# Attention, then a feed-forward network with Strassen-Winograd products: preparing the last part earlier, and a piece of a plain block kept to cover it

## The chip, the cores and the metric

The kernel runs on one core of a Trainium2 chip. The core has a matrix engine (TensorE, PE in the profile; its weight loads are PEld), a vector engine (VectorE, DVE), a scalar engine (ScalarE, ACT), a general engine (GpSimd, POOL) and an engine that only issues transfers (SyncE, SP). Each takes its instructions in its own order, and engines wait for each other by semaphores. Matrix products go into PSUM, which here has two large banks ("sc") and four small ones ("mm") in turn; everything else is kept in SBUF. The metric is the time of one execution in microseconds of device time, the median of three runs.

## The reference

64 attention heads (batch 8 x 8 heads) of 576 rows and 64 columns, in which only scores within tau of a row's largest take part, and then a feed-forward network on all 4608 rows:

```python
scores = scale * np.matmul(q, k.transpose(0, 1, 3, 2))
thresh = np.max(scores, axis=-1, keepdims=True) - tau
scores = np.where(scores >= thresh, scores, -1000000000.0)
scores = scores - np.max(scores, axis=-1, keepdims=True)
attn = np.exp(scores)
attn = attn / (np.sum(attn, axis=-1, keepdims=True) + 1e-09)
attn_out = np.matmul(attn, v)
# (B,H,S,D) -> (B*S, H*D)
x = attn_out.transpose(0, 2, 1, 3).reshape(4608, 512)
h = x @ w_in                       # 512 x 2048
g = 0.5 * h * (1.0 + erf(h / np.sqrt(2)))
out = g @ w_out                    # 2048 x 512
```

All in float32.

## The kernel before

The 4608 rows of x are 18 blocks of 256. Blocks 0 to 7 go through the network in the plain way (`block_steps`: products hT, gelu, products o_ps); their products fill PE between the scores of attention, since attention keeps DVE busy. Blocks 8 to 17 come after attention, as two groups of five blocks, in the last part: there both layers are done by the Strassen-Winograd scheme, with 7 products of quarters instead of 8, in two levels for the first layer. That needs sums of quarters of x, of the weights and of g, made by DVE and GpSimd.

Attention goes by pairs of heads (32 of them) and by 5 chunks of rows for each. A chunk's scores go into the "sc" banks (one for each head), DVE takes their maxima, ScalarE the exponentials, and DVE's last pass sets what lies under the threshold to zero and sums the rows. Only then can the next chunk's scores go in. How much of a plain block is put between is set by a table of goals, in blocks (a block is some 54.6 us of PE):

```python
GOAL = [(-1, 0.0), (START - 1, 0.0), (BATCH - 1, 0.42)]
GOAL += [(BATCH * (m + 2) + DIVIDE, x) for m, x in enumerate([1.96, 2.97, 3.98, 4.98, 5.99, 6.99])]
GOAL += [(BATCH * B + WEIGH, PLAIN)]
...
fill(1e12, B * S)          # what is left of the plain blocks, after attention
late_end.close()
last_blocks()
```

At the end of each pair the row sums are turned, inverted and spread over the partitions by way of DRAM (`divisors`), the weighted sum of v goes to x (`weigh_v`, products xT, copied by ScalarE), and GpSimd multiplies it by the inverses (`divide`):

```python
def divisors(p):
    ...
    nc.vector.transpose(turned, den)
    rows = dram.tile([4, Q, Q], FP32, tag="turned", name="turned", bufs=4)
    nc.sync.dma_start(rows.rearrange("a k i -> (a k) i"), turned)
    t = st[p]["inv"] = dg.tile([P, S], FP32, tag="inv", name="inv")
    ...                                    # four more, rows -> t, on nc.sync
```

The last part begins with the sums of x (t_x, x and, in place, xall) and of w_out (t_out); the sums of w_in (s_in, s_out, s_plain) have been issued after the last scores. What stands in `beside` is issued piece by piece, one piece after each product (`step`):

```python
x_tiles()
beside.extend(x_sums())
for _ in range(9):
    beside.pop(0)[1]()
w_out_sums(vec, 0)
```

A step (group n, quarter j of the hidden columns; 8 steps in all) does a first layer and a second. A chain of seven products adds up in its banks: m1 is evicted, m6 is added on top and evicted again, then m5, then m3, each into another quarter of the result; m7 and m4 do the same in a second bank. m5 and m3 of a chain are issued among the products of the next one (`before`).

```python
def chain(n, m, takes, done=None, runs=1):
    x, y = bank("sc", n), bank("mm", n)
    ...
    step(one_of("m1", x, True))
    step(before[0])                        # m5 of the chain before
    step(one_of("m7", y, True))
    if v is not None:
        step(one_of("m2", v, True))
    step(before[1])                        # m3 of the chain before
    step(one_of("m6", x, False))
    step(one_of("m4", y, False))
    waiting.append((one_of("m5", x, False), one_of("m3", x, False)))
```

The first layer is seven such chains of 49 products; the last two make V = c[:, 2] (g12) and U = c[:, 1] (g21), and R and W are g11 and g22:

```python
outer("a12", "b21", R, R, when(m3=lambda: (gelu_on(flat(W)), gelu_on(flat(R)))))
outer("a22", "t4", V, V, when(m3=lambda: gelu_on(flat(V))))

last = {"m2": lambda: gelu_on(U[:, 0, 0, :]), "m4": lambda: gelu_on(U[:, 1, 0, :]),
        "m5": lambda: gelu_on(U[:, 1, 1, :]), "m3": lambda: gelu_on(U[:, 0, 1, :])}
outer("s4", "b22", U, U, when(**last))
```

The second layer begins with five products of g12, among them m5 and m3 of the last chain, then come five chains of six. DVE adds each product to the output o (`taken`; in the first step of a group ScalarE copies it instead, where there is nothing yet to add to). The sums of g (8 of them, 128 x 640; the first is g21 + g22 of the first half) are issued beside:

```python
for m in range(MT):
    v = bank("mm", HD)

    def run(m=m, v=v):
        product(v, rows(g12, m, w(1, 0)), True)
        taken(lo[m][:, 0:HD], v, None if first else lo[m][:, 0:HD])

    step(run)
    if m < 2:
        step(before[m])                    # m5, then m3 of the last chain
    if m == 1:
        sums = list(g_sums())
        beside.extend(sums[:3])
        beside.extend(spread(sums[3:]))    # spread: every second step
between(-1)
for m in range(MT):
    ...
    chain(HD, ms, takes, done)
    between(m)
```

Of the kernel before, what the change touches and what calls it, by code (L numbers as in the profile page):

```python
# [18 lines left out]
def kernel(  # L19
# [28 lines left out]
    nc = tc.nc  # L48
    ctx.enter_context(tc.manual_schedule())

    B, H, S, D = q.shape
    d_model, d_ff = moe_w_in.shape
    P = 128
    Q = 32
    HP = H // 2
    NP = B * HP
    EARLY = HP
    NC = S // P
    MAIN = NC * P
# [390 lines left out]
    def divisors(p):  # L450

        den = sums[p % 2]
        n = 2 * NC + 1
        nc.vector.tensor_scalar(den[:, 0:n], den[:, 0:n], 1e-9, None, op0=ALU.add)
        nc.vector.reciprocal(den[:, 0:n], den[:, 0:n])
        turned = small.tile([P, Q], FP32, tag="turned", name="turned", bufs=2)
        nc.vector.transpose(turned, den)
        rows = dram.tile([4, Q, Q], FP32, tag="turned", name="turned", bufs=4)  # L460
        nc.sync.dma_start(rows.rearrange("a k i -> (a k) i"), turned)
        t = st[p]["inv"] = dg.tile([P, S], FP32, tag="inv", name="inv")
        flat = rows.rearrange("a k i -> a (k i)")
        for e in range(2):
            to = t[e * D:(e + 1) * D]
            src = flat[:, e * P:(e + 1) * P].unsqueeze(0).to_broadcast([D, 4, P])
            nc.sync.dma_start(to[:, 0:MAIN].rearrange("p (a x) -> p a x", x=P), src)
            src = rows[2 * e:2 * e + 2, 2 * NC, :].unsqueeze(0).to_broadcast([D, 2, Q])
            nc.sync.dma_start(to[:, MAIN:S].rearrange("p (a x) -> p a x", x=Q), src)

    def turn_p(p, i):

# [189 lines left out]
    def sub(eng, out, a, b):  # L662
        eng.tensor_tensor(out, a, b, op=ALU.subtract)  # L663
# [83 lines left out]
    def x_sums():  # L747

        room = list(tail["x_room"])
        x = xall[:, 0:len(AWAY), :, :].rearrange("p b (k h) (o t) -> p b k h o t", k=2, o=2)  # L750
        part = {f"b{k + 1}{o + 1}": x[:, :, k, :, o, :] for k in range(2) for o in range(2)}
        right = tail["right"] = {}

        def inner(eng, name, v, keep=False):
            b = {(h, i): v[:, :, h, i * RUN:(i + 1) * RUN] for h in range(2) for i in range(2)}
            t1, t2, t4 = (room.pop(0) for _ in range(3))
            t3 = room.pop(0) if keep else b[0, 1]
            right[name] = {"b11": b[0, 0], "b21": b[1, 0], "b22": b[1, 1], "t1": t1, "t2": t2, "t3": t3, "t4": t4}
            yield eng, lambda: sub(eng, t1, b[0, 1], b[0, 0])
            yield eng, lambda: sub(eng, t3, b[1, 1], b[0, 1])  # L760
            yield eng, lambda: sub(eng, t2, b[1, 1], t1)
            yield eng, lambda: sub(eng, t4, b[1, 0], t2)

        def outer(eng, out, a, b):
            yield eng, lambda: sub(eng, out, a, b)

        t1, t2, t4 = tail["t_x"]
        yield from outer(vec, t1, part["b12"], part["b11"])
        yield from inner(vec, "b11", part["b11"])
        yield from inner(vec, "t1", t1, True)  # L770
        yield from outer(vec, t2, part["b22"], t1)
        yield from inner(vec, "t2", t2, True)
        yield from outer(vec, part["b12"], part["b22"], part["b12"])
        yield from inner(vec, "t3", part["b12"])
        yield from inner(vec, "b22", part["b22"])
        yield from outer(vec, t4, part["b21"], t2)
        yield from inner(pool, "b21", part["b21"])
        yield from inner(pool, "t4", t4)
# [21 lines left out]
    def step(which):  # L800

        if which is not None:
            which()
        if beside:
            beside.pop(0)[1]()
        while beside and beside[0][0] is pool:
            beside.pop(0)[1]()
# [26 lines left out]
    def gelu_on(t):  # L834
        nc.scalar.activation(t, t, AF.Gelu)  # L835

    def layer_in(j, between):

        c, g = tail["c"], tail["g"]
        R, U, V, W, T = c[:, 0], c[:, 1], c[:, 2], c[:, 3], g[:, 0]  # L840

        def flat(t):
            return t.rearrange("p a b c -> p (a b c)")

        def outer(a, b, to, first, done=None):
            l, r = left(a, j), tail["right"][b]
            m = {"m1": ("a11", "b11"), "m2": ("a12", "b21"), "m3": ("s4", "b22"), "m4": ("a22", "t4"),
                 "m5": ("s1", "t1"), "m6": ("s2", "t2"), "m7": ("s3", "t3")}
            m = {k: [(l[p], r[q])] for k, (p, q) in m.items()}

            def at(f, t, again=False):
                d = to[:, f, t, :]
                return d, (d if again else None if first is None else first[:, f, t, :])

            takes = {"m1": [at(0, 0)], "m7": [at(1, 1)], "m6": [at(1, 0)], "m4": [at(1, 0, True)],
                     "m2": [at(0, 0, True)], "m5": [at(1, 1, True)], "m3": [at(0, 1)]}
            chain(QT, m, takes, done, len(AWAY))

        def when(**what):
            return lambda name: what[name]() if name in what else None  # L860

        def m5_out(f, t):
            return lambda: add(pool, W[:, f, t, :], V[:, f, t, :], T[:, f, t, :])

        def m5_all():
            m5_out(0, 1)()
            add(pool, flat(U), flat(U), flat(T))

        outer("a11", "b11", R, None)
        outer("s1", "t1", T, None)  # L870
        between()
        outer("s2", "t2", U, R)
        outer("s3", "t3", V, U, when(m2=m5_out(0, 0), m4=m5_out(1, 0), m5=m5_out(1, 1), m3=m5_all))
        outer("a12", "b21", R, R, when(m3=lambda: (gelu_on(flat(W)), gelu_on(flat(R)))))
        outer("a22", "t4", V, V, when(m3=lambda: gelu_on(flat(V))))

        last = {"m2": lambda: gelu_on(U[:, 0, 0, :]), "m4": lambda: gelu_on(U[:, 1, 0, :]),
                "m5": lambda: gelu_on(U[:, 1, 1, :]), "m3": lambda: gelu_on(U[:, 0, 1, :])}
        outer("s4", "b22", U, U, when(**last))

    def g_sums():

# [16 lines left out]
    def layer_out(blocks, j, between, first, final):  # L899
# [19 lines left out]
# [4 lines that stand above are left out]
                product(v, rows(g12, m, w(1, 0)), True)  # L923
                taken(lo[m][:, 0:HD], v, None if first else lo[m][:, 0:HD])

            step(run)
            if m < 2:
                step(before[m])
            if m == 1:
                sums = list(g_sums())  # L930
                beside.extend(sums[:3])
                beside.extend(spread(sums[3:]))
        between(-1)
        for m in range(MT):
            l0, l1, h0, h1 = lo[m][:, 0:HD], lo[m][:, HD:2 * HD], hi[m][:, 0:HD], hi[m][:, HD:2 * HD]
# [14 lines left out]
    def last_blocks():  # L950

        assert set(x_free) == {XSLOTS - 2, XSLOTS - 1}
        GROUPS[0].sort(key=x_at.get)
        x_tiles()
        beside.extend(x_sums())
        for _ in range(9):
            beside.pop(0)[1]()
        w_out_sums(vec, 0)
        steps = [(n, j if n % 2 == 0 else NJ - 1 - j) for n in range(len(GROUPS)) for j in range(NJ)]
        for at, (n, j) in enumerate(steps):  # L960
            before = steps[at - 1] if at else None
            after = steps[at + 1] if at + 1 < len(steps) else None

            def in_layer_in():
                if before and before[1] != j:
                    w_out_sums(pool, j)

            def in_layer_out(m):
                if after is None:
                    return  # L970
                if m == -1 and after[0] != n:
                    for k in range(2):
                        for b, x in enumerate(GROUPS[after[0]]):
                            nc.sync.dma_start(xall[:, b, 2 * k:2 * k + 2, :], away[x][:, 2 * k:2 * k + 2, :])
                if m == 0 and after[1] != j:
                    beside.append((pool, lambda j=after[1]: w_in_sums(pool, j)))
                if m == 2 and after[0] != n:
                    beside.extend(x_sums())

            layer_in(j, in_layer_in)  # L980
            layer_out(GROUPS[n], j, in_layer_out, at % NJ == 0, at % NJ == NJ - 1)
        while waiting:
            for f in waiting.pop(0):
                f()
        assert not beside
# [29 lines left out]
    START = 2 * HP + 2  # L1015

    GOAL = [(-1, 0.0), (START - 1, 0.0), (BATCH - 1, 0.42)]
    GOAL += [(BATCH * (m + 2) + DIVIDE, x) for m, x in enumerate([1.96, 2.97, 3.98, 4.98, 5.99, 6.99])]
    GOAL += [(BATCH * B + WEIGH, PLAIN)]

    def goal(n):
        for (lo, x), (hi, y) in zip(GOAL, GOAL[1:]):
# [134 lines left out]
```

## Time and profile before

| what | value |
|---|---|
| time, median of 3 | 1376.94 us (1376.78 to 1378.49) |
| span of the profiled run | 1375.6 us |
| granted clock of PE, mean | 0.992 |
| last scores of attention begin | 872.65 us |
| first product of the last part begins | 891.38 us |
| second group's first product begins | 1132.97 us |
| PE busy from 240 to 840 us | 598.85 of 600 us |
| DVE busy from 240 to 840 us | 506.57 of 600 us |

The timeline gives for each run of instructions its start and duration in us, its engine and line, what it writes and reads with the shapes, how many there are, and in square brackets how long the engine had been idle before it and on whose instruction that ended. A float32 product of the program appears as two PE records. PE's ends are modelled and reach over into the next product, so what a product costs is read from start to start. The waits give for pairs of instructions the total in us, the number of times and the longest.

### The profile page before, as it was taken

The numbers are of one execution on the slowest core, as the hardware profiler recorded it, in microseconds if no ns is written. First come the engines' busy times: TensorE is split into PE (matmuls) and PEld (weight loads), VectorE is DVE, ScalarE is ACT, GpSimd is POOL, SyncE is SP. The second block draws the span as 40 slices with busy tenths as digits, with TensorE's granted clock in tenths as the row PEclk, the third lists the DMA queues.
The fourth block names the chain that finished last, engine by engine and source line by source line (L and its number), as shares of the span: only waits on it lengthen the run. The fifth ranks groups of instructions, "written<-read, shape, count | busy, mean of one in ns | idle before, by whom it ended". The sixth has DMA issues, their size and how long they took to land.

```text
span 1375.6 us, 20037 instructions
## 1 busy us (share of the span) xinstructions
PE 1341.1 (97%) x6398; PEld 903.3 (66%) x6398; DVE 1064.8 (77%) x2054; ACT 599.6 (44%) x1000; POOL 629.3 (46%) x1080
## 2 busy tenths in 40 slices
PE   9899999999999999999999999989999999999998
PEld 6677557466466466466466476458787776877776
DVE  7998777788888888888888888883857678375665
ACT  7766537448348358358367357222201102211120
POOL 5553344455554554554554551136264403635430
PEclk9999999999999999999999999999999999999999
DMA  9987366577677687787787776500000140000003
GB/s 294 318 305 218 79 160 142 140 165 177 158 171 177 156 194 171 156 211 166 160 202 168 160 178 135 120 1 1 0 1 0 39 100 16 1 1 0 1 0 77
DMA packets 213255, 169.18 MB, mean 123 GB/s; under 512 B 114256, under 2 KB 194448, under 8 KB 213152
## 3 DMA queue, kind: packets, MB, share of 16 engines
q1 hardware_dynamic: 189200, 112.84, 37.5%
q0 software_dynamic: 23520, 54.77, 12.9%
q8 instruction: 52, 0.85, 0.3%
q14 instruction: 51, 0.42, 0.1%
q10 hardware_dynamic: 432, 0.30, 0.1%
HBM read 72.73 MB, written 12.52 MB: 62 GB/s over the span
## 4 chain that ended last, share of the span: by engine, by line
PE 87%; DVE 6%; ACT 3%; DMA 2%; issue 1%; SPq 0%; POOL 0%; ACTq 0%; DVEq 0%; POOLq 0%
PE bank L782 30%; PE hT L596 16%; PE o_ps L611 16%; PE sc L403 13%; PE xT L520 10%; PE tr L345 2%; ACT c L835 1%; DVE o L666 1%; ACT p L418 1%; DVE nmx L415 1%; DVE p L434 1%; DVE c L666 1%; DMA turned_p<-in_moe_w_in_dram 1%; DVE t_x L663 0%; DVE g L666 0%
## 5 line engine op out<-in xcount | busy, mean ns | idle before, releaser
L418 ACT ACTIVATE p<-sc,nmx 128x576 f32<-128x576 f32 x288 | 201.7, 737 | 266.9 <-DVE nmx L415 266.7
L434 DVE SCALAR_TENSOR_TENSOR p<-sc,thr,p 128x576 f32<-128x576 f32 x288 | 225.2, 815 | 62.5 <-ACT p L418 59.0
L416 POOL TENSOR_SCALAR thr<-nmx,tau_eff 128x1 f32<-128x1 f32 x288 | 89.0, 309 | 387.2 <-DVE nmx L415 386.6
L415 DVE TENSOR_REDUCE nmx<-sc 128x1 f32<-128x576 f32 x288 | 205.5, 750 | 65.5 <-PE sc L403 64.7
L596 PE MATMUL hT<-xall,w_in 128*128 128x256 f32 x1024 | 241.1, 385 | 0.0
L611 PE MATMUL o_ps<-w_out,g 128*128 128x512 f32 x512 | 237.6, 604 | 0.0
L596 PEld LDWEIGHTS hT<-xall,w_in 128*128 128x128 f32 x1024 | 189.5, 190 | 49.2 <-issue 23.8
L666 DVE TENSOR_TENSOR o<-o,bank 128x256 f32<-128x256 f32 x240 | 100.3, 419 | 106.8 <-PE bank L782 102.9
L666 DVE TENSOR_TENSOR c<-c,bank 128x320 f32<-128x320 f32 x304 | 147.2, 487 | 38.9 <-PE bank L782 23.8
L611 PEld LDWEIGHTS o_ps<-w_out,g 128*128 128x128 f32 x512 | 93.3, 190 | 111.1 <-issue 109.5
L520 PE MATMUL xT<-pT,v 128*64 128x256 f32 (+1 forms) x1280 | 163.9, 409 | 0.6 <-issue 0.6
L403 PE MATMUL sc<-kT,qT 64*128 64x288 f32 x960 | 157.5, 431 | 2.6 <-DVE p L434 2.1
L481 DVE STREAM_TRANSPOSE turned_p<-p 128x1152 f32<-128x1152 f32 x112 | 154.4, 1378 | 3.9
L403 PEld LDWEIGHTS sc<-kT,qT 64*128 64x128 f32 x960 | 89.4, 187 | 76.4 <-issue 64.8
L520 PEld LDWEIGHTS xT<-pT,v 128*64 128x64 f32 x1280 | 89.0, 137 | 73.0 <-issue 12.8
L782 PE MATMUL bank<-w_out,c 128*128 128x256 f32 x480 | 121.1, 383 | 8.0 <-ACT c L835 6.9
L265 POOL DMA_DIRECT2D v<-in_v_dram x208 | 110.8, 536 | 4.5 <-issue 2.7
L782 PEld LDWEIGHTS bank<-w_out,c 128*128 128x128 f32 x480 | 89.2, 190 | 29.3 <-ACT c L835 10.9
L835 ACT ACTIVATE c<-c 128x320 f32<-128x320 f32 (+1 forms) x56 | 44.6, 810 | 116.2 <-POOL c L666 67.8
L793 ACT COPY c<-bank 128x320 f32<-128x320 f32 x32 | 13.6, 425 | 166.3 <-PE bank L782 166.1
L782 PE MATMUL bank<-t_out,g 128*128 128x256 f32 x320 | 82.8, 381 | 1.2 <-DVE o L666 1.2
L782 PE MATMUL bank<-t_out,c 128*128 128x256 f32 x320 | 83.1, 382 | 0.0
(178 smaller groups left out, 1825.0 us busy)
## 6 DMA issues: line engine op xcount, KB each, us to landing
pT<-turned_p SPq DMA_DIRECT2D x448, 160.0 KB, 3.7
pT<-pd_tail SPq DMA_DIRECT2D x112, 80.0 KB, 3.0
q<-in_q_dram POOLq DMA_DIRECT2D x104, 72.0 KB, 3.3
k<-in_k_dram POOLq DMA_DIRECT2D x104, 72.0 KB, 3.2
inv<-turned SPq DMA_DIRECT2D x56, 128.0 KB, 3.9
v<-in_v_dram POOLq DMA_DIRECT2D x156, 40.0 KB, 3.3
out_dram<-o SPq DMA_DIRECT2D x40, 128.0 KB, 2.4
xall<-in_moe_w_out_dram POOLq DMA_DIRECT2D x9, 512.0 KB, 4.0
```

The lines of the kernel that those rows point to most:

```text
L265: eng.dma_start(t[r:P:4, e, 0:n, :], rows[:, r * KR:r * KR + n, :])
L403: nc.tensor.matmul(sc[e][:, h, 0:HALF], lhsT=lhsT, rhs=s["kT"][rows, at:at + HALF], start=True, stop=True)
L415: nc.vector.tensor_reduce(nmx[:, e:e + 1], sc, axis=AXIS.XY, op=ALU.max, negate=True)
L416: nc.gpsimd.tensor_scalar(thr[:, e:e + 1], nmx[:, e:e + 1], -1.0, tau_eff, op0=ALU.mult, op1=ALU.subtract)
L418: nc.scalar.activation(w[:, e * S:(e + 1) * S].rearrange("p (h s) -> p h s", h=2), sc, AF.Exp, bias=nmx[:, e:e + 1], scale=1.0)
L434: nc.vector.scalar_tensor_tensor(row, sc[e][:, :, 0:HALF], thr[:, e:e + 1], row, op0=ALU.is_ge, op1=ALU.mult, accum_out=den[e])
L481: nc.vector.transpose(turned_p[:, :, i // 2, 0:NB, i % 2 * Q:(i % 2 + 1) * Q], w.rearrange("p (e b i) -> p e b i", e=2, i=Q))
L520: nc.tensor.matmul(to, lhsT=s["v"][:, e, c, :], rhs=rhs, start=(c == 0), stop=(c == KR - 1))
L596: nc.tensor.matmul(hT[:, j % 2, :], lhsT=w_in_sb[c][:, j * P:(j + 1) * P], rhs=x_blk[n][:, c, :], start=(c == 0), stop=(c == N_DM - 1))
L611: nc.tensor.matmul(o[:, 0:d_model], lhsT=g[j][:, m * P:(m + 1) * P], rhs=w_out_sb[j], start=(j == 0), stop=(j == N_DF - 1))
L666: eng.tensor_tensor(out, a, b, op=ALU.add)
L782: nc.tensor.matmul(to, lhsT=l, rhs=r, start=start and k == 0, stop=k == len(pairs) - 1, skip_group_check=not start)
```

## The change

It has five pieces. The last pair's divisors are issued by GpSimd's queue, as SyncE's is full of transfers there. The goals of the plain blocks are lower, so that 0.28 of the last plain block is left for after attention, where its products can run while the sums for the last part are made; these are all issued ahead of the last part, not piece by piece between its products. The gelu of g12 is done in four quarters, each as soon as it is complete. The first sum of g is issued before the first product of the second layer. And the second group's x sums are issued from the second row of products on, not from the fourth, with each large one (`outer`) in two halves.

```diff
+        eng = nc.gpsimd if p == NP - 1 else nc.sync
         rows = dram.tile([4, Q, Q], FP32, tag="turned", name="turned", bufs=4)
-        nc.sync.dma_start(rows.rearrange("a k i -> (a k) i"), turned)
+        eng.dma_start(rows.rearrange("a k i -> (a k) i"), turned)
 ...                                       (the four others likewise)
         def outer(eng, out, a, b):
-            yield eng, lambda: sub(eng, out, a, b)
+            for h in range(2):
+                yield eng, lambda h=h: sub(eng, out[:, :, h, :], a[:, :, h, :], b[:, :, h, :])
 ...
-        outer("a22", "t4", V, V, when(m3=lambda: gelu_on(flat(V))))
-
-        last = {"m2": lambda: gelu_on(U[:, 0, 0, :]), "m4": lambda: gelu_on(U[:, 1, 0, :]),
-                "m5": lambda: gelu_on(U[:, 1, 1, :]), "m3": lambda: gelu_on(U[:, 0, 1, :])}
-        outer("s4", "b22", U, U, when(**last))
+
+        def gelus_of(to):
+            return when(**{m: lambda f=f, t=t: gelu_on(to[:, f, t, :])
+                           for m, f, t in (("m2", 0, 0), ("m4", 1, 0), ("m5", 1, 1), ("m3", 0, 1))})
+
+        outer("a22", "t4", V, V, gelus_of(V))
+        outer("s4", "b22", U, U, gelus_of(U))
 ...
+            if m == 0:
+                sums = list(g_sums())
+                sums.pop(0)[1]()
             step(run)
             if m < 2:
                 step(before[m])
             if m == 1:
-                sums = list(g_sums())
-                beside.extend(sums[:3])
-                beside.extend(spread(sums[3:]))
+                beside.extend(sums[:2])
+                beside.extend(spread(sums[2:]))
 ...
-        beside.extend(x_sums())
-        for _ in range(9):
-            beside.pop(0)[1]()
+        sums = list(x_sums())
+        for _, run in sums[:10]:
+            run()
         w_out_sums(vec, 0)
+        for _, run in sums[10:]:
+            run()
 ...
-                if m == 2 and after[0] != n:
+                if m == 0 and after[0] != n:
                     beside.extend(x_sums())
 ...
-    GOAL += [(BATCH * (m + 2) + DIVIDE, x) for m, x in enumerate([1.96, 2.97, 3.98, 4.98, 5.99, 6.99])]
-    GOAL += [(BATCH * B + WEIGH, PLAIN)]
+    GOAL += [(BATCH * (m + 2) + DIVIDE, x) for m, x in enumerate([1.92, 2.89, 3.86, 4.82, 5.79, 6.75])]
+    GOAL += [(BATCH * B + WEIGH, PLAIN - 0.28)]
```

More of the change, by code (lines that the diff above doesn't have):

```diff
@@ L466, in divisors @@
             src = flat[:, e * P:(e + 1) * P].unsqueeze(0).to_broadcast([D, 4, P])
-            nc.sync.dma_start(to[:, 0:MAIN].rearrange("p (a x) -> p a x", x=P), src)
+            eng.dma_start(to[:, 0:MAIN].rearrange("p (a x) -> p a x", x=P), src)
             src = rows[2 * e:2 * e + 2, 2 * NC, :].unsqueeze(0).to_broadcast([D, 2, Q])
-            nc.sync.dma_start(to[:, MAIN:S].rearrange("p (a x) -> p a x", x=Q), src)
+            eng.dma_start(to[:, MAIN:S].rearrange("p (a x) -> p a x", x=Q), src)
     def turn_p(p, i):
```

## The prediction

> **What bounds the kernel now.** I read the page first, then the waits of the matrix engine (PE) alone, then its timeline wherever those waits fall. The page gives PE 97% busy:
>
> ```profile
> PE 1341.1 (97%) x6398; PEld 903.3 (66%) x6398; DVE 1064.8 (77%) x2054; ACT 599.6 (44%) x1000; POOL 629.3 (46%) x1080
> ```
>
> No matmul is removed by this change, so all it can win is time in which PE stands still or runs at a lower clock: 1375.6 - 1341.1 = 34.5 us of idle, and some of that is the start. The waits of PE, each with its total, its count and its longest:
>
> ```profile
> PE bank L782 <- ACT c L835: 6.9, 8, 0.9
> PE tr L345 <- ACT diag L448: 5.7, 2, 3.6
> PE bank L782 <- DVE c L666: 5.4, 1, 5.4
> PE sc L403 <- DVE p L434: 3.0, 4, 1.6
> PE bank L782 <- DVE o L666: 3.0, 9, 0.7
> ```
>
> Rows 1, 3 and 5 lie in the last part (line 782), and the change aims at them. Row 2 is the start and stays. Row 4 is attention. The timeline of PE at the hand-over from attention to the last part:
>
> ```profile
> 895.15 0.70 PE L782 MATMUL bank<-x,s_out 128*128 128x320 f32 x2
> 895.69 0.70 PE L782 MATMUL bank<-t_x,s_out 128*128 128x320 f32 x2
> 901.83 1.43 PE L782 MATMUL bank<-xall,s_plain 128*128 128x320 f32 x2 [5.44 <-DVE c L666]
> 903.06 1.27 PE L782 MATMUL bank<-x,s_in 128*128 128x320 f32 x2
> 904.12 1.27 PE L782 MATMUL bank<-x,s_out 128*128 128x320 f32 x2
> ```
>
> A product normally starts 0.54 us after the one before it. Here one starts 6.14 us after (5.6 lost), and the next ones step by 1.07 until 907.3: 901.83 to 907.92 is 6.09 us for six steps that cost 3.24 (2.85 lost). One more gap at 908.85 loses 0.39. Sum 8.8 us. The timeline where a first layer of the last part goes over into its second:
>
> ```profile
> 1100.04 0.70 PE L782 MATMUL bank<-x,s_out 128*128 128x320 f32 x2
> 1101.61 1.13 PE L782 MATMUL bank<-w_out,c 128*128 128x256 f32 x4 [0.87 <-ACT c L835]
> 1102.57 0.70 PE L782 MATMUL bank<-x,s_in 128*128 128x320 f32 x2
> 1103.11 1.03 PE L782 MATMUL bank<-w_out,c 128*128 128x256 f32 x4
> 1103.97 0.70 PE L782 MATMUL bank<-xall,s_in 128*128 128x320 f32 x2
> ...
> 1099.74 2.17 ACT L835 ACTIVATE c<-c 128x320 f32<-128x320 f32 x3 [2.02 <-DVE c L666]
> ...
> 1102.77 0.42 DVE L666 TENSOR_TENSOR o<-o,bank 128x256 f32<-128x256 f32 x1 [1.46 <-PE bank L782]
> 1103.31 0.49 DVE L666 TENSOR_TENSOR c<-c,bank 128x320 f32<-128x320 f32 x1
> ```
>
> PE could start at 1100.04 + 0.54 = 1100.58 and starts at 1101.61: 1.03 lost, plus 0.1 for a slower first product. ScalarE is then in the 1.27 us gelu of g12, which it began after a small one. DVE stands idle 1.46 us before 1102.77. This occurs in each of the 8 steps.
>
> [...] 1.07 us for each product after the 5.44 us wait, 0.54 otherwise; the waits of 0.9 us show no such thing. [...] a gelu of 128x320 takes 0.47 us and one of 128x1280 takes 1.27, so four take 1.88. [...] SyncE issues 16 + 1 + 4 transfers from 867.0 to 884.3 while the divisors have been ready since 877.6.
>
> **The change part by part.**
>
> *Part of a block behind attention.* I counted in the order of instructions what fills PE between one chunk's scores and the next, before and after, at 0.427 us for an hT product and 0.854 for an o_ps product (20 records, two for each product, go from 873.62 to 882.16): 14.5 us less before the last scores, and the same 14.5 us more after them, 9 + 21 products of o_ps instead of 10 + 3. PE's work is the same. What counts is what it waits for. The last part then starts 14.5 us later after the last scores, 33 us instead of 18.7. In that time DVE must finish the sums of weights and x, now all issued ahead. It is through with the weight sums, the first x sums and t_out 20.2 us after the last scores (892.9 - 872.65). It then needs the last divisors: issued by GpSimd right at the transposed sums, with 0.54 us for each issue and some 3.5 us to land twice, about 14 us after the last scores; then the copies of the last xT at about 16 us and GpSimd's division (1.7 to 2.5 us), so 18.4: no wait. What remains for DVE is three large sums of 1.5 us and twelve of 0.45: 9.9 us. Done at 30.1, 3 us ahead of PE. So the 5.6, the 2.85 and the 0.39 go: **-8.8 us**.
>
> *Does attention give the 14.5 us back in full?* A score product can only start when DVE is through with the former scores. Two lines of the timeline, of DVE and of PE, in the middle of attention:
>
> ```profile
> 575.65 0.81 DVE L434 SCALAR_TENSOR_TENSOR p<-sc,thr,p 128x576 f32<-128x576 f32 x1
> ...
> 572.00 1.24 PE L403 MATMUL sc<-kT,qT 64*128 64x288 f32 x8
> 573.17 3.70 PE L611 MATMUL o_ps<-w_out,g 128*128 128x512 f32 x8
> 576.80 1.24 PE L403 MATMUL sc<-kT,qT 64*128 64x288 f32 x8
> ```
>
> A slot of two heads with 3.42 us of filling takes PE 4.8 us, and DVE's last pass ends at 576.4, 0.4 us before the next scores; the one-head slot ends level at 2.56 us of filling and loses 0.5 at 2.13. I went through the slots of all 27 later pairs with these margins. The filling taken away comes mostly from slots with 3.84 or 4.27 us; four one-head slots gain filling, three fall to 2.13 or 1.71. The waits add up to 3.3 us before and 4.6 after: **+1.3 us**.
>
> *The gelu in four.* Of g12, three quarters are now done before the chain's last product, and the first product of the second layer reads two of these only. The wait of 1.03 and the slow 0.1 go in 8 steps: **-8.8 us**. ScalarE has over 2 us idle there.
>
> *First sum of the second layer sooner.* It now stands in DVE's queue ahead of the first output and of the eviction of m5, and waits for ScalarE's gelu of a g21 quarter. That quarter's add ends 0.74 us after the chain's last product, its gelu 0.5 later, the sum (0.73) at 2.03, the first output at 2.36, m5's eviction at 2.85. PE wants to add m3 into the same bank 0.86 + 0.54 + 0.86 = 2.26 us after the chain's last product, so it waits about 0.6 us, with 0.1 for a slow restart, where today it doesn't wait. That is a new wait in 6 steps; in the first step of each group the first output is evicted by ScalarE and it is about 0.3: +4.2 + 0.6 = +4.8. In return the later sums are one shorter on DVE: a regular step loses 2.0 us now (58.58 from step to step, against 49 x 0.538 + 35 x 0.863 = 56.57), 1.1 of it the gelu and 0.9 DVE's backlog; I give it back 0.3 in 6 steps, -1.8. Together **+3.0 us**.
>
> *Second group's sums sooner.* Between 1123 and 1145 PE loses 0.78, 0.25, 0.91, 0.25 and 0.43 us in gaps, as x sums and evictions share DVE; beginning them two rows of products earlier puts 23 of 28 under products of 0.863 us, where DVE has room (0.33 + 0.40), and leaves 5 among those of 0.54. The new x is there: its transfers run from 1104.7 to about 1111.4, the sums would begin at about 1113. Of 2.6 us I take **-2.2 us**.
>
> Sum: -8.8 + 1.3 - 8.8 + 3.0 - 2.2 = -15.5 us; 1376.9 - 15.5 = 1361.4, taken as **1361 us**.
>
> **The rivals.**
> 1. *The new wait doesn't occur*: DVE's early sum finds its gelu done, or m3 isn't held by it. For it: DVE idles 1.46 us there today. Against: the order of instructions puts the sum ahead of the eviction that m3 needs. Then 4.8 us more are won: about 1356 us.
> 2. *DVE becomes the bound of attention.* A pair needs some 23.9 us of DVE with its inevitable waits and 24.2 to 24.6 of PE after the change. For it: the margin in two-head slots is only 0.4 us. Against: pairs with 13.24 us of filling exist already and lose 0.5 at most. If each of 23 pairs lost another 0.3 us: 1368 us.
> 3. *The last part starts as late as before*, because the last division or a transfer from GpSimd comes late, or the moved block waits for its gelus: then 5 to 9 us aren't won, 1366 to 1370 us. Against it: 3 us of margin.
> 4. *Only shifted waits in the first layer*: freed of the gelu, PE runs into DVE's backlog at m6 (today a 0.43 us wait) sooner; I have that in the sum.
>
> **Range and chances.** Rivals 1 and 2 are the likeliest errors and pull in opposite directions: 1354 to 1368 us. 2% is 27.5 us, thus below 1349.4; even with all 34.5 us of idle the start's part (8.7 us in the first 100 us) can't be won, and it would take every gap of the last part: 3%. Slower by 2% would need something that no row speaks for: 2%.
>
> **What would show it.** The wait of PE for DVE c of 5.4 us gone, and no step of 1.07 us after the hand-over; the 8 waits for ACT c gone; in their place a wait of about 0.6 us between the first two outputs and m3, six times, put down to DVE c; the sum of PE's waits for DVE p in attention up by 1 to 2 us; the steps of the last part at about 57.9 us instead of 58.6. I am wrong if the hand-over still shows a gap over 2 us, if attention loses over 4 us to DVE, or if the steps of the last part come down below 57.2.

## The result, and the profile after

| | before | changed kernel |
|---|---|---|
| time, median of 4 runs each, taken together | 1377.72 us (1376.78 to 1379.61) | 1368.24 us (1366.25 to 1369.28) |
| ratio | | 0.9928, 95% interval 0.9911 to 0.9945 |
| span of the profiled run | 1375.6 us | 1365.8 us |
| last scores begin | 872.65 us | 860.17 us |
| last scores to first product of the last part | 18.7 us | 36.35 us, 14.5 of it the moved work |
| last part, first product to the end | 484.3 us | 469.3 us |

The change wins 9.5 us, 0.7%. The prediction was 15.5 us won and 1361 us: 6 us more than came, and the result lies at the upper edge of its range, 1354 to 1368 us. The page's first lines, with the busy time of each engine, and then the waits of PE (total, count, longest):

```profile
PE 1338.9 (98%) x6398; PEld 904.1 (66%) x6398; DVE 1066.8 (78%) x2062; ACT 600.3 (44%) x1024; POOL 634.4 (46%) x1085
```

```profile
PE sc L403 <- DVE p L434: 4.4, 6, 1.6
PE bank L784 <- DVE c L667: 2.8, 6, 0.5
...
PE xT L521 <- DMA pT<-pd_tail: 2.2, 1, 2.2
```

Line 784 is the line 782 of before, 667 the line 666. The eight waits for ScalarE's c are gone from the list, and so is the single one of 5.4 us. "DVE c" is now something else, six short waits; and the last row is new, where the kernel before has 0.6 us put down to no instruction. The timeline of the hand-over, where "POOL ... inv<-turned" are GpSimd's transfers of the divisors and "SPq ... pT<-pd_tail" SyncE's transfers of the last pair's tails:

```profile
866.98 4.02 SPq L500 DMA_DIRECT2D pT<-pd_tail  x4
868.82 0.65 POOL L468 DMA_DIRECT2D inv<-turned  x1 [2.74 <-issue]
868.96 3.34 PE L521 MATMUL xT<-pT,v 128*64 128x320 f32 x22
...
874.47 3.36 PE L521 MATMUL xT<-pT,v 128*64 128x256 f32 x18 [2.18 <-DMA pT<-pd_tail]
877.76 18.92 PE L612 MATMUL o_ps<-w_out,g 128*128 128x512 f32 x42
...
896.52 0.70 PE L784 MATMUL bank<-xall,w_in 128*128 128x320 f32 x2
897.06 0.70 PE L784 MATMUL bank<-xall,s_plain 128*128 128x320 f32 x2
```

From 896.52 on the products step by 0.54 us without a gap: the gap *in* the last part is gone. But PE stands still for 2.18 us ahead of the moved work, and the 18 records behind that take 3.29 us. The granted clock there is 0.69 (874.40 to 877.70). The same 18 take 2.27 us at a clock of 1.00, as in sum_after_m5 below. The change of layer (PE and DVE of one window):

```profile
978.27 0.70 PE L784 MATMUL bank<-x,s_out 128*128 128x320 f32 x2
978.81 1.03 PE L784 MATMUL bank<-w_out,c 128*128 128x256 f32 x4
...
979.67 0.70 PE L784 MATMUL bank<-x,s_in 128*128 128x320 f32 x2
980.09 0.82 DVE L667 TENSOR_TENSOR g<-c 128x640 f32<-128x640 f32 x1 [0.54 <-ACT c L837]
980.21 1.03 PE L784 MATMUL bank<-w_out,c 128*128 128x256 f32 x4
980.83 0.41 DVE L667 TENSOR_TENSOR o<-o,bank 128x256 f32<-128x256 f32 x1
981.16 0.48 DVE L667 TENSOR_TENSOR c<-c,bank 128x320 f32<-128x320 f32 x1
...
981.70 0.81 PE L784 MATMUL bank<-xall,s_in 128*128 128x320 f32 x2 [0.46 <-DVE c L667]
```

The first product of the second layer now starts 978.81 - 978.27 = 0.54 us after the last one of the first layer: no wait for the gelu. But at 980.09 DVE takes the early sum of g, which waited for a gelu until then; the output and the eviction of m5 (981.16) queue behind it; and m3 at 981.70 starts 1.49 us after the product before it instead of 0.86.

Added up over the two profiles, in starts: until 138 us the changed run is 1.1 us ahead (from run to run the start differs by more: the scores near 167 us begin at 164.82 us in old_goals and at 167.98 in sum_after_m5); attention loses 3.1; the hand-over up to the last part loses 3.1 over the moved work; the last part wins 15.0. Sum -9.9 us, and the spans differ by 9.86. So nearly the whole of what was expected of the last part came (16.8 expected there), and 6 us were given back ahead of it, where I had expected 1.3.

### The profile page after: what moved, and what is told of

Read it like the earlier page. It is cut to its first block, busy times and chain, and to the rows that moved or that the text cites. A ratio compares the mean times of both kernels' runs of the same rounds, so it can differ in the third digit from the quotient of the medians.

```text
span 1365.8 us, 20074 instructions
## 1 busy us (share of the span) xinstructions
PE 1338.9 (98%) x6398; PEld 904.1 (66%) x6398; DVE 1066.8 (78%) x2062; ACT 600.3 (44%) x1024; POOL 634.4 (46%) x1085
## 4 chain that ended last, share of the span: by engine, by line
PE 84%; DVE 8%; DMA 3%; SPq 2%; ACT 1%; issue 1%; POOL 0%; DVEq 0%; ACTq 0%; POOLq 0%
PE bank L784 30%; PE hT L597 16%; PE o_ps L612 15%; PE sc L403 12%; PE xT L521 10%; PE tr L345 1%; DVE o L667 1%; DMA turned_p<-in_moe_w_in_dram 1%; DVE nmx L415 1%; DVE p L434 1%; DVE c L667 1%; DMA x<-xall 1%; DVE c L664 1%; DVE power L217 1%; ACT p L418 1%
## 5 line engine op out<-in xcount | busy, mean ns | idle before, releaser
L667 POOL TENSOR_TENSOR c<-c,g 128x320 f32<-128x320 f32 (+1 forms) x40 | 50.5, 1271 | 79.1 <-DVE c L667 79.1
```

Of the source, the lines that this page charges most:

```text
L667: eng.tensor_tensor(out, a, b, op=ALU.add)
```

## The experiments

Three numbers are compared in all runs. *Last part*: from its first product to the end. *Hand-over*: from the last scores to the last part, less the plain work moved there, against before. *Attention*: the start of the last scores against that of the scores near 167 us, less the filling between them, against before. A fresh run of the changed kernel shows how far these repeat; the ratios are all to the kernel before.

**after_again**: the changed kernel as it is.

> The changed kernel once more, as the measure for its variants on the same chip. Expected: 0.993 of the kernel before, some 9 to 10 us less; the wait of PE for the transfers of pd_tail at the hand-over again near 2 us.

1365.84 us, ratio 0.9922 (0.99 to 0.9945). Last part 469.27 us, as before to 0.01. Attention +2.7 and hand-over +1.75, against +3.1 and +3.1. The wait for the tails is there again, 1.8 us, but behind it PE runs at full rate: the 42 o_ps records take 18.1 us to the next start instead of 18.8. So what the last part shows is exact to hundredths; the hand-over differs by 1.4 us between these two profiles, and attention by 2.6 over the eight profiles that share it (below).

### What each piece brings

**gelu_alone**: the kernel before with only the gelus in quarters.

```diff
-        outer("a22", "t4", V, V, when(m3=lambda: gelu_on(flat(V))))
 ...
-        outer("s4", "b22", U, U, when(**last))
+        outer("a22", "t4", V, V, gelus_of(V))
+        outer("s4", "b22", U, U, gelus_of(U))
```

> The kernel before with the gelu of g12 in four quarters and nothing else. Theory (the eight waits for the large gelu are paid in full and nothing takes their place): the gaps of 1.03 us ahead of the second layers go, 8 to 9 us less than before, 1368 to 1369 us, as much as the whole change brings. Rival (PE freed of it runs into DVE's backlog at once): gaps at m6 and m4 grow by some 0.5 us in each step, 4 us less than before, 1373 us.

1369.77 us, ratio 0.9938 (0.9922 to 0.9954). Last part 475.53 us against 484.26: 8.7 us won, with the waits ahead of the second layer gone in all 8 steps, and the gap at the hand-over still there (9.2 us in the first layer). This one piece brings 7.2 us, where the whole change brings 9.5 and 11.1 in its two runs.

**cover_alone**: the kernel before with only the lower goals and all x sums ahead of the last part; divisors on SyncE.

```diff
-        beside.extend(x_sums())
-        for _ in range(9):
-            beside.pop(0)[1]()
+        sums = list(x_sums())
+        for _, run in sums[:9]:
+            run()
         w_out_sums(vec, 0)
+        for _, run in sums[9:]:
+            run()
 ...                                       (and the goals of the change)
```

> The kernel before with only the two edits at the hand-over: all weight and x sums ahead of the last part and the plain work behind the last scores; the gelus in one piece, the group sums in one piece and at their old places. Theory: the 8.95 us gap within the last part goes to 0.1 or less, attention loses 1 to 3 us, and 1 to 3 us are lost at the transfers of the last pair, so 4 to 7 us are won: 1370 to 1373 us. The last part's first bank product to the end goes from 484.3 to about 475.4. Rival: the hand-over gives everything back and the total is within 2 us of the kernel before, above 1375 us.

1371.94 us, ratio 0.9959 (0.9943 to 0.9976). Last part 475.32 us: 8.94 won, all of the gap. Attention +2.7. But the loss expected at the hand-over did not come: -0.5 us, with a wait of 0.2 us at the tails. So what is lost there in the changed kernel doesn't come from the cover.

**old_goals**: the changed kernel with the goals of before, so that nothing is left to cover the sums.

```diff
-    ... enumerate([1.92, 2.89, 3.86, 4.82, 5.79, 6.75])]
-    GOAL += [(BATCH * B + WEIGH, PLAIN - 0.28)]
+    ... enumerate([1.96, 2.97, 3.98, 4.98, 5.99, 6.99])]
+    GOAL += [(BATCH * B + WEIGH, PLAIN)]
```

> The changed kernel with the pace of the plain work as it was before, so that the 14.5 us of TensorE work lie within attention again and nothing covers the sums and divisors behind the last scores. Theory: that cover is worth the whole hand-over. Attention then ends about where the kernel before ends it, the last scores start near 872 us, and about 14 us of TensorE idle or waiting time appear between the last scores and the first product of the last part, because all sums now stand ahead of it and are done some 30 us after the last scores. So last scores to the first product takes 30 to 33 us instead of 35 to 36, attention gains back 2 to 3 us, and the total is 9 to 13 us above the changed kernel, near 1376 us. Rival: the hand-over gap came only from VectorE's order at the first evictions, so the order of the sums alone removes it, and the total stays within 3 us of the changed kernel.

1375.29 us, ratio 0.9982 (0.9975 to 0.9989): 7 to 9.5 us above the changed kernel's two runs, with 9 to 13 expected. The cover is what removes the gap, and not the order of the sums; but I had the place of the idle time wrong. PE starts the last part after 21.7 us, not after 30 to 33, since its first nine products need only what is there, and then it waits for an eviction that stands in DVE's queue behind the sums (PE's timeline):

```profile
892.77 0.70 PE L784 MATMUL bank<-xall,w_in 128*128 128x320 f32 x2
...
897.08 0.70 PE L784 MATMUL bank<-t_x,s_out 128*128 128x320 f32 x2
904.18 1.43 PE L784 MATMUL bank<-xall,s_plain 128*128 128x320 f32 x2 [6.41 <-DVE c L667]
```

It is the gap of before over again, 9.4 us with the steps of 1.07 us behind it, and it lies four microseconds into the last part. Attention, at the goals of before, loses only 0.4.

### The early sum of g

**late_first_sum**: the changed kernel with the sums of g where the kernel before has them.

```diff
-            if m == 0:
-                sums = list(g_sums())
-                sums.pop(0)[1]()
             step(run)
 ...
             if m == 1:
-                beside.extend(sums[:2])
-                beside.extend(spread(sums[2:]))
+                sums = list(g_sums())
+                beside.extend(sums[:3])
+                beside.extend(spread(sums[3:]))
```

> The changed kernel with the first sum of g issued where it was before. Theory (this sum ahead of m5's eviction makes m3 wait): the gaps between the first two outputs and m3, 0.62 us in six steps and 0.29 in two, fall to 0.1; the gaps at m6 and m4 stay at about 0.6; some 3 us less, 1365 us. Rival (the sums only change places, and DVE's backlog at m6 and m4 grows by as much as m3 gains): gaps of 1.2 us there and the same time, 1368 us.

1361.0 us, ratio 0.9885 (0.9864 to 0.9906). Last part 464.5 us instead of 469.27. The waits ahead of m3 (0.62 us in six steps, 0.29 in two) are zero, and so is the slow 0.1 behind them; DVE's backlog later in the layer is the same 0.62 in six steps with the early sum and without it. What the early sum does return is a gap of 0.1 us further on in each of the 8 steps, 0.8 us in all. Net it costs 4.8 us, more than the 3 expected.

**sum_after_m5**: the changed kernel with the first sum issued two evictions later, behind that of m5.

```diff
-            if m == 0:
-                sums = list(g_sums())
-                sums.pop(0)[1]()
             step(run)
             if m < 2:
                 step(before[m])
+            if m == 0:
+                sums = list(g_sums())
+                sums.pop(0)[1]()
```

> The changed kernel with only the first group sum issued later: after the eviction that the next product waits for, not ahead of it. Theory: the new wait between v0's products and the next ones (0.6 us in six steps and 0.3 in two) falls to 0.1 or less, no other gap grows by more than 0.1 a step, and the last part takes 464.5 us as with the sums at their old place. Total 1361 to 1363 us. Rival: the sum only moves the wait one eviction further on, so that a new gap of 0.4 to 0.6 us a step shows there and the last part stays at 468 to 469 us.

1363.13 us, ratio 0.9895 (0.9877 to 0.9912). Last part 464.12 us. The same stretch, PE and DVE:

```profile
981.65 0.42 DVE L667 TENSOR_TENSOR o<-o,bank 128x256 f32<-128x256 f32 x1 [0.32 <-PE bank L784]
981.99 1.03 PE L784 MATMUL bank<-w_out,c 128*128 128x256 f32 x4
982.19 0.49 DVE L667 TENSOR_TENSOR c<-c,bank 128x320 f32<-128x320 f32 x1
982.60 0.82 DVE L667 TENSOR_TENSOR g<-c 128x640 f32<-128x640 f32 x1
982.85 0.70 PE L784 MATMUL bank<-xall,s_in 128*128 128x320 f32 x2
```

The eviction of m5 (982.19) goes ahead of the sum (982.60), and m3 starts at 982.85, 0.86 us after the product before it, with no wait at all. Two places in DVE's order are worth 5.1 us over eight steps. The rival, that the wait would only move on by one eviction, falls.

### The hand-over

**sync_divisors**: the changed kernel with the last pair's divisors on SyncE, as before.

```diff
-        eng = nc.gpsimd if p == NP - 1 else nc.sync
+        eng = nc.sync
```

> The changed kernel with the last pair's divisors issued by SyncE again. Theory (the transfers that GpSimd issues run at the same time as those of pd_tail and hold them up): PE's wait for pd_tail falls from 2.2 us to about 1, the half clock after it goes, the last part begins some 2.5 to 3 us sooner, about 1365 us; the divisors come some 5 us later and x sums on DVE end still before the last part. Rival (pd_tail is late only because SyncE's queue is full and PE comes sooner): the wait stays at 2 us and the time at 1368; second rival (the late divisors hold up the sums): a wait for DVE at the hand-over, 1370 us or more.

1365.56 us, ratio 0.991 (0.9896 to 0.9925). Hand-over -0.6 us, and no wait at the tails (PE and SyncE in one window):

```profile
869.82 3.25 SPq L500 DMA_DIRECT2D pT<-pd_tail  x4
871.69 5.81 PE L521 MATMUL xT<-pT,v 128*64 128x320 f32 x40
...
875.28 0.61 SPq L468 DMA_DIRECT2D inv<-turned  x1
...
877.42 18.29 PE L612 MATMUL o_ps<-w_out,g 128*128 128x512 f32 x42
```

All 40 records of xT run through. The divisors come 6.5 us later here (875.28 against 868.82, with the last scores 2.7 us later), and nothing waits for them: DVE still is idle for 2.7 us before its first eviction of the last part. The total is the changed kernel's all the same, as attention lost 4.1 us in this profile and the start 1.7 more; the hand-over itself is seen only in its own stretch.

**swap_queues**: divisors on SyncE, tails on GpSimd.

```diff
-        eng = nc.gpsimd if p == NP - 1 else nc.sync
+        eng = nc.sync
 ...
-                nc.sync.dma_start(by_64(s["pT"][e])[:, 2 * NC, :, at:at + Q], pd_tail[p % 2][rows])
+                eng = nc.gpsimd if p == NP - 1 else nc.sync
+                eng.dma_start(by_64(s["pT"][e])[:, 2 * NC, :, at:at + Q], pd_tail[p % 2][rows])
```

> The changed kernel with the last pair's queues exchanged: the divisors' transfers from SyncE, the tails' transfers from GpSimd. Theory: [...] the wait for the tails, 1.8 to 2.2 us, goes; the divisors land in time because some 20 us of moved work cover them. Last scores to the first product of the last part takes 32.5 to 33.5 us, against 36.4 and 35.0 in two runs of the changed kernel; the total 2 to 3 us below it. Rival: GpSimd is at the sums and issues the tails late, so that the wait for the tails grows beyond 2.2 us and the total is equal or worse.

1365.9 us, ratio 0.9916 (0.9897 to 0.9934). Last scores to last part 32.75 us, hand-over -0.5, no wait at the tails. The 2 to 3 us expected don't show in the total, as attention lost 4.6 us in this profile. It does not matter here which engine issues the tails. In all profiles the long wait goes with the divisors' four broadcasts (inv<-turned) beside them:

| kernel | divisors' broadcasts issued by | waits of PE within xT, us | hand-over, us |
|---|---|---|---|
| before, gelu_alone | SyncE, after the tails | 0.6; 0 | 0; -0.7 |
| changed kernel, two runs | GpSimd, beside the tails | 2.2; 1.8 + 0.4 | +3.1; +1.75 |
| late_first_sum, sum_after_m5, away_pool | GpSimd, beside the tails | 1.5 + 0.9; 2.0; 1.8 | +1.9; +1.3; +1.1 |
| old_goals | GpSimd, beside the tails | 2.1 | +3.0 |
| sync_divisors, cover_alone | SyncE, after the tails | 0; 0.2 | -0.6; -0.5 |
| swap_queues, best2, best3 | SyncE, after the tails, which GpSimd issues | 0; 0; 0.2 | -0.5; -0.7; -0.5 |
| best1 | the same, and blocks put away by GpSimd | 0.7 + 0.5 | 0.0 |

The two largest, +3.1 and +3.0, have in common that PE went on slower behind the wait: the changed kernel takes 3.29 us for 18 records of xT, at a clock of 0.69, and old_goals 4.36 us for 20, where sum_after_m5 takes 2.27 us for 18 at 1.00. The 1.5 us in late_first_sum are put down to a copy of ScalarE, not to the tails. The 1.2 us of best1 stay unexplained: its last block was put away at 692 us, and the broadcasts came after the tails. In the six profiles with long waits GpSimd is always the issuer too; the divisors from SyncE at the earlier time were not run, so issuer and time are not separated.

### Attention

**away_pool**: the changed kernel with the finished x blocks put away to DRAM by GpSimd's queue.

```diff
     def put_away(n):
 ...
-        nc.sync.dma_start(away[n], x_blk.pop(n))
+        nc.gpsimd.dma_start(away[n], x_blk.pop(n))
```

> The changed kernel with one edit: the transfers that put finished x blocks away to DRAM are issued by GpSimd instead of SyncE. In the changed kernel ScalarE waits 15 us for these transfers before it can copy the next xT products, against 5.7 us in the kernel before and 5.8 with the earlier pace of plain work. Theory: SyncE issues them behind a long line of other transfers, and part of attention's 3 us come from this wait, which the lower goals have moved onto the path; then the wait falls below 6 us and attention gains about 1.5 us, total 1365 to 1367 us. Rival: the transfer itself is slow to land or GpSimd issues it no sooner, so that the wait stays at 10 us or more and the total stays as it is.

1365.2 us, ratio 0.9907 (0.9891 to 0.9923). Attention +0.3 instead of +2.7 and +3.1. First the changed kernel near 600 us, with xT's products, the put-away, ScalarE's copies and exponentials, DVE's last pass and the scores that wait for it:

```profile
593.86 5.07 PE L521 MATMUL xT<-pT,v 128*64 128x320 f32 x40
...
595.89 1.51 SPq L650 DMA_DIRECT2D x<-xall  x1
...
596.82 0.32 ACT L531 COPY xall<-xT 128x192 f32<-128x192 f32 x1 [0.66 <-PE xT L521]
...
601.40 0.43 ACT L531 COPY xall<-xT 128x128 f32<-128x128 f32 x2 [4.26 <-DMA x<-xall]
...
603.74 0.27 ACT L531 COPY xall<-xT 128x128 f32<-128x128 f32 x1 [1.91 <-DMA x<-xall]
603.90 1.38 ACT L418 ACTIVATE p<-sc,nmx 128x576 f32<-128x576 f32 x2
...
604.75 0.82 DVE L434 SCALAR_TENSOR_TENSOR p<-sc,thr,p 128x576 f32<-128x576 f32 x1 [2.57 <-ACT p L418]
...
605.72 1.21 PE L403 MATMUL sc<-kT,q_tail 128*128 128x288 f32 x4 [1.34 <-DVE p L434]
```

and with GpSimd's queue:

```profile
585.54 0.60 POOL L650 DMA_DIRECT2D x<-xall  x1 [0.18 <-POOL thr L416]
...
592.96 0.57 POOL L650 DMA_DIRECT2D x<-xall  x1
593.16 5.07 PE L521 MATMUL xT<-pT,v 128*64 128x320 f32 x40
...
596.12 0.49 ACT L531 COPY xall<-xT 128x192 f32<-128x192 f32 x2 [0.66 <-PE xT L521]
...
598.31 0.43 ACT L531 COPY xall<-xT 128x128 f32<-128x128 f32 x2 [1.70 <-PE xT L521]
```

GpSimd sends the first block at 585.5, so it was ready by then; SyncE, in its order behind other transfers, issues it at 595.9. ScalarE wants to copy new xT into those places at 596.8 and waits 4.26 and 1.91 us. The exponentials queue behind the copies, DVE behind the exponentials, and at 605.72 PE waits 1.34 us "for DVE p". With GpSimd's queue the copies wait for PE alone. In the kernel before the same transfer was issued no earlier, but there the copies came 3.5 us behind it, and waited 0.7 and 1.2 us:

```profile
605.75 1.02 SPq L649 DMA_DIRECT2D x<-xall  x2
...
609.25 0.30 ACT L530 COPY xall<-xT 128x192 f32<-128x192 f32 x1
```

The lower goals have taken out the plain work that used to lie between. The rows of waits say it for the whole span. In the changed kernel (ScalarE's waits) it is

```profile
ACT xall L531 <- DMA x<-xall: 15.4, 4, 5.5
```

against 5.7 us in the kernel before and 5.8 in old_goals; with GpSimd's queue the row is gone, and PE's waits for DVE have shrunk with it:

```profile
PE sc L403 <- DVE p L434: 1.8, 2, 1.6
```

One of these is a wait of 1.58 us early in attention that the kernel before and the changed kernel have too. Over all profiles: the change's goals with SyncE's put-away, 8 profiles, +2.7 to +5.3 us; the goals of before, +0.4 and (gelu_alone) +1.8; the change's goals with GpSimd's put-away, +0.3 and +1.0. The ratio's interval overlaps that of the changed kernel, so the time of this run alone would not show it; the waits do, and best1 against best2 below shows it in the time as well.

### Put together

**best2**: the changed kernel with the edits of sum_after_m5 and swap_queues.

> The changed kernel with two mendings: first group sum issued after the eviction of m5, and queues of the last pair exchanged; blocks put away from SyncE as in the change. Theory: the two terms add, last part 464.1 us and last scores to last part 32.7 us: 1360 to 1361.5 us. Rival: the hand-over's gain is lost again, so the total stays at 1363 us, where the sum alone has brought it.

1360.51 us, ratio 0.9873 (0.9859 to 0.9888). Last part 464.05, last scores to last part 32.5 us: each of the two keeps what it won in its own stretch.

**best1**: best2 with the blocks put away by GpSimd.

> The changed kernel with all three mendings: first group sum issued after the eviction of m5, queues of the last pair exchanged, blocks put away from GpSimd. Theory: the terms add, last part 464.1 us, last scores to last part 32.7 us, attention 1.5 us better: 1359 to 1360 us. Rival: the put-away from GpSimd gives nothing, 1361 us.

1357.69 us, ratio 0.9857 (0.9841 to 0.9874). Attention +1.0 instead of +3.9; PE's waits for DVE p 2.2 us instead of 4.9. It is 2.8 us below best2, where I had expected 1.5; the hand-over gives 0.7 of it back.

**best3**: best2 with 0.20 of a block kept instead of 0.28.

```diff
-    ... enumerate([1.92, 2.89, 3.86, 4.82, 5.79, 6.75])]
-    GOAL += [(BATCH * B + WEIGH, PLAIN - 0.28)]
+    ... enumerate([1.93, 2.91, 3.89, 4.86, 5.85, 6.81])]
+    GOAL += [(BATCH * B + WEIGH, PLAIN - 0.2)]
```

> best2 with less of the plain block kept for the time behind attention: 0.20 of a block instead of 0.28, some 10.4 us of TensorE work instead of 14.5. Theory: the sums are done about 31.9 us after the last scores and TensorE runs some 4 us ahead of its first needed eviction, so 10.4 us still cover them: last scores to last part about 28.7 us, no gap behind it, and attention loses a third less to VectorE, so the total is 0.5 to 1.5 us below best2. Rival: the cover is too short, a wait for VectorE of 1 to 3 us comes back in the first products of the last part, and half clock with it: 1 to 4 us above best2.

1357.4 us, ratio 0.985 (0.9835 to 0.9864). Last scores to last part 28.5 us, no gap behind it: 10.2 us of cover are enough. Attention +0.7: the copies here come 2.1 us behind the put-away (601.26 and 599.17) instead of 1.1 in best2, and ScalarE waits 9.1 us for it instead of 16.2. That is 3.1 us below best2, more than the 0.5 to 1.5 expected, and level with best1. Both are some 20 us below the kernel before, and 8 to 11 below the change. Less cover and GpSimd's put-away together were not run.

## Why the prediction was right, and where it was short

*The hand-over, -8.8.* Right within the last part: the gap measured 8.95 us and is gone, in the changed kernel and in cover_alone, which has this piece alone. Right too in the sums: expected done 30.1 us after the last scores, measured 31.7, and DVE then stood idle for 6.5 us. Short in one term: I took the way to the last part as work only, "33 us instead of 18.7". It took 36.35 and 35.0. The step that failed is what I made of SyncE's 21 transfers from 867.0 to 884.3, with the divisors ready since 877.6: that an issue by GpSimd would only save time was my estimate, and no run showed it. The prediction asked whether the divisors would land in time and not what they would delay. In six profiles with the divisors beside the tails PE waits 1.8 to 2.4 us there, in seven with the divisors after the tails 0.6 at most, and 1.2 in best1. Behind a cover of 14.5 us the divisors were in no hurry (sync_divisors), so this piece of the change costs 1.7 to 3.7 us at the hand-over, against sync_divisors, and brings nothing. Where on the way the delay arises is not shown. The prediction's own sign of being wrong, a gap over 2 us at the hand-over, did come (2.18 us), but ahead of the moved work and not in the last part; and of rival 3 a part came true, a late start of the last part, by way of the tails and not of the division.

*Attention, +1.3.* Measured +3.1 and +2.7. The step that failed is the account of what a slot waits for: it used DVE's margin alone, and took the row "sc <- DVE p" for DVE being short of time. That row rose from 3.0 to 4.4 us, within the 1 to 2 us named as a sign, so the sign came by luck, from another cause. away_pool has the same goals and the same DVE work, and loses 0.3 us (best1 1.0). So most of the loss is the put-away behind SyncE's other transfers, which reaches PE by way of ScalarE and DVE. In the kernel before, this wait of ScalarE was there to be read, 5.7 us on its own list; the prediction read PE's list only. Rival 2, DVE as the bound of attention, falls with it.

*The gelu in four, -8.8.* Right: gelu_alone wins 8.7 us in the last part.

*First sum sooner, +3.0.* The wait was right: 0.6 us in six steps and 0.3 in two were predicted, 0.62 and 0.29 came, with the slow 0.1 behind, put down to DVE c. What failed is the size of the return, "I give it back 0.3 in 6 steps, -1.8": DVE's backlog of 0.62 us in six steps stayed, and only 0.1 a step came back, 0.8 in all. The term is +4.8 (late_first_sum), and rival 1 does not occur. The prediction treated the backlog as a sum of DVE's work. Here it was an order: which eviction stands behind which sum.

*Second group, -2.2.* The gaps between its first rows and the next first layer went from 2.7 to 1.7 us: -1.0. The sums did move under the longer products, but the first two halves ran beside GpSimd (below) and took longer; that this is what is missing was not tested. The steps of the last part came to 58.05 us, with 57.9 expected.

With the measured terms the sum is -8.95 + 3.1 (tails and clock) + 3.1 - 8.7 + 4.8 - 1.0 = -7.65, and 1.1 in the last part that no single term accounts for and 1.1 from the start make the 9.9 of the spans. So the mechanisms held in the last part, where two sizes were off; ahead of it one wait was missing and the other had the wrong cause. All four errors lie in one direction: what the change moves work *onto* was counted too cheap each time.

## What to carry to other kernels

When work is moved, list the waits of the engines and queues *behind* the bound engine too, here ScalarE's wait for a transfer that had been hidden by the very work that was moved; a row "PE waits for DVE" names only the last link. Issuing the divisors from a free engine, and so sooner, was not free here (1.7 to 3.7 us at the hand-over): ask what lands at the same time and whether the one made sooner was needed sooner. And in front of an engine in order, place each new instruction behind the eviction that the bound engine needs next: the same sum cost 5.1 us two places earlier than there.

## What the runs showed of the hardware

*DVE and GpSimd slowed each other.* The timeline of swap_queues (DVE and GpSimd), DVE's four sums of w_out (t_out, all 128x512, between SBUF tiles) beside GpSimd's division and first subtraction:

```profile
880.91 2.61 POOL L546 TENSOR_TENSOR xall<-xall,inv 128x64 f32<-128x64 f32 x3 [8.26 <-DMA inv<-turned]
881.73 1.21 DVE L665 TENSOR_TENSOR t_out<-w_out 128x512 f32<-128x512 f32 x1
882.97 1.10 DVE L665 TENSOR_TENSOR t_out<-w_out,t_out 128x512 f32<-128x512 f32 x1
883.49 1.31 POOL L665 TENSOR_TENSOR xall<-xall 128x320 f32<-128x320 f32 x1
...
883.99 1.35 DVE L665 TENSOR_TENSOR t_out<-w_out 128x512 f32<-128x512 f32 x1
...
885.26 0.68 DVE L665 TENSOR_TENSOR t_out<-w_out,t_out 128x512 f32<-128x512 f32 x1
...
898.25 0.87 POOL L665 TENSOR_TENSOR xall<-t_x 128x320 f32<-128x320 f32 x1
```

Beside GpSimd a sum takes 1.10 to 1.35 us, and after it 0.68. GpSimd's subtraction takes 1.31 beside DVE's sums; one of the same shape takes 0.87 at 898.25, and 0.86 at 894.35 in the changed kernel, where DVE has nothing from 891.93 to 898.41. In sum_after_m5, where GpSimd's subtraction ends at 883.20, all four sums, from 883.46 on, take 0.68 or 0.69. Not every overlap costs as much: in sync_divisors the sums begun at 880.56 and 881.28 kept their 0.69, with GpSimd's division on the trace from 880.91. In the changed kernel the first two t_x halves of the second group (1107.49 and 1109.23) took 1.48 and 1.15 us beside GpSimd instead of the 0.82 of a later one (1116.93).

*Half clock after a short wait.* Behind a wait of 2.18 us the changed kernel has a granted clock of 0.69, behind one of 1.98 us sum_after_m5 has 1.00. The stretch behind the wait in each, with its clock third from the end:

```profile
874.40:877.70 3.30, 3.23 (x18) 1.89 (x18) 3.23 (x7) 0.00 (x0) 1.43 (x2) 0.69 0.00 0
```

```profile
878.20:880.50 2.30, 2.21 (x18) 1.54 (x18) 2.23 (x5) 0.00 (x0) 1.56 (x2) 1.00 0.00 0
```

From 875.6 to 879.0 us the clock was 0.51 in the changed kernel. It lost 1.65 us more on the same records of xT and o_ps (3.29 + 18.76 against 2.27 + 18.13 us, from start to start), nearly as much again as the wait. So a wait of 2.18 us cost 3.83 here, and the 1.98 us of sum_after_m5 cost nothing more: the length alone does not decide, since behind the 1.58 us near 158 us the clock was 0.50 as well (158.9 to 162.2, changed kernel). What does decide is not shown.
